# Three of a first tile's six transposing loads on ScalarE's queue, and a plan with other constants

## The chip, the core and the metric

The kernel runs on one core of a Trainium2 chip. The core's engines each run their own instruction stream, in order: TensorE (PE, with its weight loads as PEld), VectorE (DVE), ScalarE (ACT), GpSimd (POOL) and SyncE (SP). An engine waits on semaphores that other engines and the DMA transfers raise. SyncE and ScalarE can each issue DMA transfers from their own queue. The metric is the device time of one execution in microseconds (us).

## The reference

A speech codec's forward pass, in bfloat16: a depthwise convolution over time with three taps, SiLU, four stages of residual vector quantization with eight codes each, and a second depthwise convolution over the sum of the chosen codes. Shapes: x is 2 x 16000 x 512, dw_enc and dw_dec are 3 x 512, codebooks are 4 x 8 x 512.

```python
z = jnp.zeros_like(x)
for i in range(K):
    z = z + xp[:, i:i+T, :] * dw_enc[i][None, None, :]
z = _silu(z)
res = z
q = jnp.zeros_like(z)
for s in range(Nq):
    cb = codebooks[s]
    d2 = (jnp.einsum("btd,btd->bt", res, res)[..., None]
          - 2.0 * jnp.einsum("btd,cd->btc", res, cb)
          + jnp.einsum("cd,cd->c", cb, cb)[None, None, :])
    idx = d2.argmin(-1)
    sel = cb[idx]
    q = q + sel
    res = res - sel
qp = jnp.pad(q, ((0,0),(pad,pad),(0,0)))
y = jnp.zeros_like(x)
for i in range(K):
    y = y + qp[:, i:i+T, :] * dw_dec[i][None, None, :]
```

## The kernel before

**Tiles.** Each of the two sequences of 16000 rows is cut into nine tiles (SIZES, line 230): G = 6, 8 and seven of 16 groups of 128 rows for the first sequence, the mirror image for the second, 18 tiles in all. A tile's x lies in SBUF transposed, channels on the partitions, in one of two buffers XT (NX = 2): slot g + 1 holds the rows of group g, and slots 0 and G + 1 hold the neighbours that the convolution needs at the edges.

**Loading a tile** (load, lines 487 to 510). One transposing DMA for each of the G slots, all issued by SyncE (line 493). The edge slots of most tiles are two more such loads (lines 501 and 507), so a tile of 16 groups takes 18. For the first tile GpSimd makes the edge slots from slots G and 1 with two copies (lines 504 and 510).

**Setup** (lines 344 to 485). ScalarE's queue issues three small loads: the encoder weights WER, the codebooks CB1, and dw_dec, broadcast to all partitions. TensorE transposes WER, and VectorE copies it out as WENC, which the taps need. From the codebooks come their transposes CBT and CBM2 (ScalarE), Gram matrices and block tables BD (VectorE), and the stationary operands CBN; from dw_dec and the codebooks the decoder's tables WDEC. VectorE also clears a good many buffers at the start.

**One tile's work.** front (line 514): in each of two halves of the channels, three taps multiplied on ScalarE (line 531) or VectorE (line 532), two additions on VectorE, exp and reciprocal on ScalarE, and the product on VectorE (SiLU). select (line 582): scores on TensorE and decisions on VectorE for the first three stages. resid (line 681): the chosen codes are taken off z by TensorE products, and the result goes back to SBUF by ScalarE (line 707) or VectorE (line 709); then the fourth stage. back (line 741): the decoder as products on TensorE, copied out by ScalarE (line 766) and stored by SyncE (line 789).

**The order.** Nothing is scheduled by hand. Every step is registered with `add`, with its engine, a cost, a key of three numbers and what it reads and writes. `Plan.order` then simulates the engines with these costs: again and again it takes the step that can start earliest, and among steps that can start at the same time the one of the lowest rank. The rank is w[0] + key[1] + w[1] * key[2], with w from the table WHEN by the step's name and the part of the run (the first three tiles, the middle, the last three). The program's instructions are issued in that order, so it is each engine's order. A "tail" is the time from the end of a step's issue to its landing, as the plan counts it. SHARE and SLACK decide, where ScalarE and VectorE can both do a step, which of them does. The costs shape the order alone: the time on the chip is the chip's.

The DMA transfers share eight semaphores (numbers 101 to 108 in the trace), handed out in turn by the framework under the kernel. A transfer that gets a semaphore waits until that semaphore's earlier transfer has landed.

Of the kernel before, what the change touches and what calls it, by code (L numbers as in the profile page):

```python
# [12 lines left out]
ACT = mybir.ActivationFunctionType  # L13
# [3 lines left out]
class Plan:  # L17
# [9 lines left out]
    SPAN, BUSY = 3.413, 0.5  # L27
    GATE = {"resid": (1.0, 2.0), "back": (1.0, 2.0), "win0": (0.6, 1.5), "win3": (0.6, 1.5), "score0": (0.25, 1.4), "score3": (0.25, 1.4)}

    def __init__(self, pairs, edges, share, slack, quota, when):  # L30
        self.steps, self.writer, self.readers = [], {}, {}
        self.pairs, self.edges, self.share, self.slack, self.quota, self.when = pairs, edges, share, slack, quota, when

    def add(self, engine, cost, key, fn, reads=(), writes=(), take=None, free=None, hold=None, tail=0.0, after=(), dest=None, box=None, mm=0):
        n = len(self.steps)
# [18 lines left out]

    def rank(self, s):
        w = self.when[s["k"][0]][self.part(s)]
        return w[0] + s["k"][1] + w[1] * s["k"][2]

    def product(self, t, c, share, half):

# [14 lines left out]
    def order(self):  # L75
# [8 lines left out]
        at = [0.0] * len(steps)  # L84
        clock = {e: 0.0 for e in self.LATENCY}
        waiting = {e: [] for e in clock}
        held = {e: 0 for e in clock}
        banks = [0.0] * (2 * self.pairs)
# [4 lines left out]
        out = []  # L93
# [9 lines left out]
        def load(d, t):  # L103
            return max(clock[d] - t, 0.0) + held[d] + sum(cost(steps[m], d) for m in waiting[d]
                                                        if at[m] <= t + 1.0 and (d == "DVE" or not isinstance(steps[m]["e"], tuple)))
# [8 lines left out]
        def look(s, e):  # L114

            t = max(at[s["n"]], clock[e])
            if s["take"]:
                dest = s["dest"]
                if dest == "ANY":
                    full = [d for d in ("ACT", "DVE") if held[d] >= self.quota[d]]  # L120
                    if len(full) == 2:
                        return inf, None
                    if full:
                        dest = "ACT" if full[0] == "DVE" else "DVE"
                    else:
                        dest = "DVE" if load("DVE", t) + self.share[self.part(s)] < load("ACT", t) else "ACT"
                elif dest and held[dest] >= self.quota[dest]:
                    return inf, None
                kind = s["take"][0]
                t = place(kind[dest] if isinstance(kind, dict) else kind, t)[0]  # L130
                return t + late(many(s, dest), t, cost(s, dest) if s["dest"] == "ANY" else s["c"]), dest
            if isinstance(s["e"], tuple) and e == "ACT" and t + s["c"]["ACT"] > max(at[s["n"]], clock["DVE"]) + s["c"]["DVE"] + self.slack[self.part(s)]:
                return inf, None
            if s["mm"]:
                t += late(s["mm"], t, s["c"])
            return t, None
# [9 lines left out]
        while len(out) < len(steps):  # L146
            (t, dest), _, n, e = min(((look(steps[n], e), rank[n], n, e) for e, names in waiting.items() for n in names),
                                     key=lambda q: (q[0][0], q[1], q[2], q[3]))
            assert t < inf
            s = steps[n]  # L150
            for w in waiting.values():
                if n in w:
                    w.remove(n)
            c = cost(s, dest if s["take"] and s["dest"] == "ANY" else e)
            s["fill"] = None
            if s["mm"] and s["k"][0] != "setup":
                j = min(range(2 * self.pairs), key=lambda j: (banks[j], j))
                since = max(clock["PE"], banks[j])
                k = 0
                while t - clock["PE"] > self.AFTER and since + self.REST + self.FILL * (1 if self.full else 2) < t:  # L160
                    since = self.product(since, self.FILL, 1.0, 2.0)
                    k += 1
                if k > 0:
                    s["fill"] = (j, k)
                    run += k
                    if run > self.CHUNK:
                        run -= self.CHUNK
                        fetched = t + self.FETCH
            if s["take"]:
                kind, box = s["take"]  # L170
                kind = kind[dest] if isinstance(kind, dict) else kind
                j = place(kind, t)[2]
                box["banks"] = [j, j + 1] if kind == "A" else [j]
                for j in box["banks"]:
                    banks[j] = inf
                box["dest"] = dest
                if s["dest"] == "ANY":
                    steps[n + 1]["e"] = dest
                if dest:
                    held[dest] += 1  # L180
            elif s["box"] is not None:
                s["box"]["dest"] = e
            if s["hold"] and table != s["hold"]:
                table = s["hold"]
                c += self.TABLE
            if s["mm"]:
                m = many(s, dest)
                c = self.product(t, c, *self.GATE.get(s["k"][0], (0.5, 1.5))) - t
                run += m
                if run > self.CHUNK:  # L190
                    run -= self.CHUNK
                    fetched = t + c * (m - run) / m + self.FETCH
            s["t"], s["d"], s["on"] = t, c, e
            clock[e] = t + c
            self.busy[e] += c
            end = t + c + s["tail"]
            if s["free"]:
                if s["free"]["dest"]:
                    held[s["free"]["dest"]] -= 1
                for j in s["free"]["banks"]:  # L200
                    banks[j] = end + self.LATENCY[e]
            out.append(s)
            for u in users[n]:
                ue = steps[u]["e"]
                at[u] = max(at[u], t + c + self.AGAIN[e] if ue == e else end + self.LATENCY[e])
                left[u] -= 1
                if not left[u]:
                    open_(u)
# [5 lines left out]
def kernel(  # L214
# [8 lines left out]
    nc = tc.nc  # L223
# [18 lines left out]
    PAIR = 1  # L242
    NX, NE, NZ, NOH, NY = 2, 3, 4, 4, 4
    NA = 4
    SHARE = (19.5, 1.71, -1.34)
    SLACK = (0.8, -4.83, -5.72)
    QUOTA = {"ACT": 4, "DVE": 4}
    WHEN = {"setup": ((-0.05, 1.675), (0.613, 1.016), (0.464, 0.931)), "load": ((-2.074, 0.741), (-2.063, 0.601), (-2.58, 0.741)),
            "pad": ((-1.343, 0.11), (-1.736, 0.115), (-2.291, 0.134)), "taps": ((0.284, 0.643), (-0.413, 0.648), (0.441, 1.172)),
            "exp": ((0.672, 0.139), (0.624, 0.043), (0.853, 0)), "plus1": ((1.287, 0.521), (0.349, 0.234), (0.268, 0.646)),  # L250
            "recip": ((0.542, 0.819), (0.469, 0.213), (1.361, 0.627)), "gate": ((-0.104, 0.712), (0.552, 0.521), (1.523, 0.809)),
            "score0": ((-0.134, 0), (0.889, 0), (-0.19, 0)), "decide": ((1.83, 0.266), (-0.088, 0.293), (0.366, 0.69)),
            "win0": ((2.039, 0), (2.077, 0), (2.756, 0)), "resid": ((1.585, 0.742), (1.683, 0.632), (1.826, 0.993)),
            "score3": ((2.285, 1.086), (2.738, 0.327), (2.939, 1.624)), "decide3": ((1.327, 0.17), (2.815, 0.429), (3.624, 0.724)),
            "win3": ((3.135, 0.143), (3.003, 1.197), (2.818, 0.209)), "back": ((2.723, 0.576), (3.156, 1.159), (4.372, 0.628))}
    assert B == len(SIZES) and T >= GM * P and GM <= 16

    xf = x.flatten_outer_dims()
# [7 lines left out]
    tiles = []  # L266
    for b, sizes in enumerate(SIZES):
        done = 0
        for g in sizes:
            r = g * P  # L270
            t0 = max(0, min(done - 2, T - r))
            end = T if t0 + r >= T else t0 + r - 2
# [11 lines left out]
    CB1 = sb([NC, D], BF16, "CB1")  # L284
# [37 lines left out]
    CBN = {(s, u): sb([P, D], BF16, f"CBN{s}_{u}") for s in range(3) for u in range(2)}  # L322
    WDEC = [sb([P, D], BF16, f"WDEC{v}") for v in range(4)]

    plan = Plan(NA, (3, len(tiles) - 3), SHARE, SLACK, QUOTA, WHEN)
    add = plan.add

    def ps(box):
# [14 lines left out]

    wd_rows = bass.AP(tensor=dw_dec.tensor, offset=dw_dec.offset, ap=[[0, P], [D, K], [1, D]])
    add("ACT", 0.6, ("setup", -9, 0), lambda: nc.scalar.dma_start(out=WER, in_=dw_enc.rearrange("k (i p) -> (k i) p", p=P)), writes=["WER"], tail=1.6)
    add("ACT", 0.6, ("setup", -9, 0), lambda: nc.scalar.dma_start(out=CB1, in_=codebooks.flatten_outer_dims()), writes=["CB1"], tail=2.2)
    def load_wd():
        with nc.allow_non_contiguous_dma(reason="small weights"):
            nc.scalar.dma_start(out=WDBC, in_=wd_rows)
    add("ACT", 0.4, ("setup", -8, 0), load_wd, writes=[("Y", 3)], tail=5.5)  # L350
    add("POOL", 2.0, ("setup", -30, 0), lambda: make_identity(nc, IDENT), writes=["I"])

    def pool_memset(t, v, tok, cost, key):
# [133 lines left out]
    def load(st):  # L487
        n, G = st["n"], st["G"]
        X = XT[n % NX]
        src = xf[st["row0"]:st["row0"] + G * P, :].rearrange("(p g) d -> g p d", g=G)  # L490

        def one(g):
            nc.sync.dma_start_transpose(out=X[:, :, g + 1, :], in_=src[g])
        for g in range(G):
            add("SP", 1.56 if n < 2 else 1.36, ("load", n, 0.01 * g), lambda g=g: one(g), [], [("X", n % NX, g + 1)], tail=1.5)
        key = ("pad", n - 20 * (n == 0), 0)
        xe, xo = [("XE", n % NX)], [("X", n % NX, G + 1)]
        r0, t0 = st["row0"], st["row0"] % T
# [348 lines left out]
```

## Time and profile before

| | us |
|---|---|
| median of 8 runs | 731.6 |
| lowest and highest of the 8 | 729.9 and 734.07 |
| profiled execution, its time | 729.9 |
| the same, span from the first to the last instruction | 728.1 |
| VectorE busy in the first 100 us | 84.09 |
| VectorE busy from 100 to 700 us | 575.8 |
| VectorE busy in the last 28.1 us | 15.12 |

A profile row of the timeline gives the start in us from the span's start, the duration, the engine, the line of the kernel, the operation, what it writes and reads, and how many instructions are merged into the row; in brackets, how long the engine was idle before it and what ended the wait. "SPq" and "ACTq" are instructions of SyncE's and ScalarE's sequencers, DMA issues among them; their duration is that of the issue, and the landing comes later. A row of the view by stretches gives the stretch, its length, the busy time of each engine with its count, the granted clock of TensorE, the share of time that the 16 DMA engines were busy, and GB/s.

### The profile page before, as it was taken

Reading aid. Unit: us, or ns where it says so; the run is one execution under the profiler, and the core shown is the slowest. Engines: PE = TensorE matmul, PEld = TensorE weight load, DVE = VectorE, ACT = ScalarE, POOL = GpSimd, SP = SyncE. Lnnn points to the kernel's source line nnn. Section 1 sums busy time; section 2 is a strip of 40 time slices with the busy share of each in tenths; the row PEclk is TensorE's granted clock in tenths of the full one; section 3 lists DMA queues with packets and bytes.
Section 4 is the critical chain, followed back from the end, with each engine's and each line's share of the span. In section 5 each row is a group of like instructions: output and inputs, shape, how many; then the busy total and the mean of one; then the engine's idle time right before and its main releaser. Section 6 shows DMA issues by size and latency. Waiting matters only on the chain.

```text
span 728.1 us, 24317 instructions
## 1 busy us (share of the span) xinstructions
PE 584.0 (80%) x10656; PEld 288.7 (40%) x10725; DVE 675.0 (93%) x1258; ACT 658.5 (90%) x583; POOL 10.4 (1%) x35
## 2 busy tenths in 40 slices
PE   5977676887887886888787788877788897889995
PEld 2443243343443443434343434433444343444442
DVE  8779899999999999999999999999999999999993
ACT  6888998699999999899989999999899999999656
POOL 2000000000010000000000000000000010000000
PEclk9999899999999999999999999989999999999999
DMA  5444455525154353736544444542535141302316
GB/s 112 94 95 95 100 113 103 132 67 94 31 147 91 107 90 96 125 79 146 105 110 96 139 74 109 127 90 60 96 110 139 55 131 23 120 2 88 117 32 212
DMA packets 163968, 71.89 MB, mean 99 GB/s; under 512 B 155567, under 2 KB 155599, under 8 KB 163862
## 3 DMA queue, kind: packets, MB, share of 16 engines
q1 hardware_dynamic: 163646, 69.90, 40.7%
q8 instruction: 84, 1.38, 0.8%
q10 hardware_dynamic: 216, 0.43, 0.2%
q14 instruction: 22, 0.18, 0.1%
HBM read 0.43 MB, written 32.77 MB: 46 GB/s over the span
## 4 chain that ended last, share of the span: by engine, by line
DVE 53%; PE 28%; issue 8%; ACT 8%; DMA 2%; ACTq 0%; DVEq 0%
DVE ZB L709 12%; PE ps L701 8%; DVE ZB L364 7%; PE ps L700 7%; DVE TA L364 7%; DVE TB L532 7%; PE ps L567 5%; DVE TA L532 3%; DVE EX L539 3%; PE ps L758 3%; DVE OHW L678 2%; ACT YB L766 2%; PE ps L809 2%; ACT ZB L707 2%; ACT EX L549 1%
## 5 line engine op out<-in xcount | busy, mean ns | idle before, releaser
L701 PE MATMUL ps<-OHW,CBN 128*128 128x512 bf16 (+1 forms) x768 | 268.1, 386 | 20.6 <-DVE ZB L709 10.7
L707 ACT CAST ZB<-ps 128x1024 bf16<-128x1024 f32 (+2 forms) x296 | 253.4, 934 | 31.8 <-PE ps L701 30.1
L700 PE MATMUL ps<-ZB,IDENT 128*128 128x512 bf16 (+1 forms) x530 | 205.6, 388 | 31.6 <-ACT ZB L707 13.9
L709 DVE TENSOR_TENSOR ZB<-ZB,ps 128x1024 bf16<-128x1024 bf16 (+2 forms) x136 | 142.8, 1061 | 4.8 <-PE ps L701 4.3
L701 PEld LDWEIGHTS <-CBN 128*128 128x128 bf16 x768 | 74.7, 99 | 142.4 <-issue 77.0
L766 ACT CAST YB<-ps 128x1024 bf16<-128x1024 f32 x126 | 121.8, 1043 | 9.0 <-PE ps L762 4.2
L537 ACT ACTIVATE EX<-ZB 128x4096 bf16<-128x4096 bf16 (+2 forms) x36 | 115.1, 3197 | 8.5 <-DVE ZB L364 8.1
L549 ACT ACTIVATE EX<-EX 128x4096 bf16<-128x4096 bf16 (+2 forms) x36 | 114.7, 3195 | 0.2
L567 PEld LDWEIGHTS <-ZB 128*32 128x32 bf16 x8064 | 75.1, 95 | 54.9 <-issue 52.3
L567 PE MATMUL ps<-ZB 128*32 128x64 bf16 x8064 | 87.4, 197 | 8.3 <-issue 5.6
L532 DVE TENSOR_SCALAR TB<-XT,WENC 128x2048 bf16<-128x2048 bf16 (+2 forms) x139 | 92.4, 683 | 0.2
L809 PE MATMUL ps<-MSK,IDENT 128*128 128x512 bf16 x277 | 70.4, 401 | 14.9 <-issue 2.5
L758 PE MATMUL ps<-WDEC,OHW 128*128 128x512 bf16 x219 | 68.0, 387 | 14.7 <-DVE ZB L709 4.6
L700 PEld LDWEIGHTS <-IDENT 128*128 128x128 bf16 x530 | 53.0, 100 | 66.9 <-issue 14.8
L364 DVE TENSOR_TENSOR ZB<-ZB,EX 128x4096 bf16<-128x4096 bf16 (+2 forms) x36 | 72.6, 2018 | 3.6 <-ACT EX L549 3.6
L364 DVE TENSOR_TENSOR TA<-TA,TB 128x4096 bf16<-128x4096 bf16 (+2 forms) x36 | 72.7, 2020 | 1.0 <-ACT TB L531 0.6
L364 DVE TENSOR_TENSOR ZB<-TA,TB 128x4096 bf16<-128x4096 bf16 (+2 forms) x36 | 72.6, 2017 | 0.1
L532 DVE TENSOR_SCALAR TA<-XT,WENC 128x2048 bf16<-128x2048 bf16 (+2 forms) x70 | 46.7, 687 | 0.9 <-DMA out_dram<-YB 0.4
L809 PEld LDWEIGHTS <-IDENT 128*128 128x128 bf16 x294 | 28.8, 102 | 46.5 <-issue 18.7
L539 DVE TENSOR_SCALAR EX<-EX 128x4096 bf16<-128x4096 bf16 (+2 forms) x35 | 38.4, 1096 | 1.2 <-ACT EX L537 1.2
L758 PEld LDWEIGHTS <-OHW 128*128 128x128 bf16 x252 | 22.8, 98 | 41.5 <-issue 18.3
L672 PE MATMUL ps<-IDENT,OHA 128*32 128x128 bf16 x504 | 21.5, 223 | 9.8 <-DVE OHA L364 4.8
(100 smaller groups left out, 394.4 us busy)
## 6 DMA issues: line engine op xcount, KB each, us to landing
out_dram<-YB SPq DMA_DIRECT2D x33, 448.0 KB
out_dram<-YB SPq DMA_DIRECT2D x28, 512.0 KB
XT<-in_x_dram SPq DMA_TRANSPOSE x283
out_dram<-YB SPq DMA_DIRECT2D x30, 60.0 KB
out_dram<-YB SPq DMA_DIRECT2D x31, 2.0 KB
out_dram<-YB SPq DMA_DIRECT2D x2, 224.0 KB
YB<-in_dw_dec_dram ACTq DMA_DIRECT2D x1, 384.0 KB
out_dram<-YB SPq DMA_DIRECT2D x1, 384.0 KB
```

The costliest lines, as they stand in the source:

```text
L364: add("DVE", cost, key, lambda: nc.vector.tensor_tensor(out=out, in0=a, in1=b, op=op), reads, writes, **kw)
L532: lambda dst=dst, src=src, w=w: nc.vector.tensor_scalar(out=dst, in0=src, scalar1=w, scalar2=None, op0=ALU.mult),
L537: add("ACT", act(2 * R), ("exp", n, h), lambda: nc.scalar.activation(v(ex), Z, ACT.Exp, scale=-1.0), zt, [("EX", sl), "ACTTAB"], hold="E")
L549: nc.scalar.add_instruction(mybir.InstActivation(name=nc.get_next_instruction_name(), engine=mybir.EngineType.Activation, func=ACT.Reciprocal,
L567: nc.tensor.matmul(o[HB * q:HB * (q + 1), u * ZW:(u + 1) * ZW].rearrange("p (s c) -> p s c", s=2), lhsT=blk, rhs=both, start=False, stop=( ...
L700: nc.tensor.matmul(o, lhsT=IDENT, rhs=zg[:, k0:k0 + nk, :], start=True, stop=False)
L701: nc.tensor.matmul(o, lhsT=CBN[s, u][:, i * P:(i + 1) * P], rhs=W[:, k0:k0 + nk, PADC:PADC + P], start=not on_act, stop=True)
L707: nc.scalar.copy(zg, v)
L709: nc.vector.tensor_tensor(out=zg, in0=zg, in1=v, op=ALU.add)
L758: nc.tensor.matmul(o, lhsT=W[:, k, PADC:PADC + P], rhs=WDEC[u], start=True, stop=not wrap)
L766: add("ACT", act_psum(1024), key, lambda k=k, box=box, Y=Y, k0=k0: nc.scalar.copy(Y[:, 2 * (k - k0):2 * (k - k0) + 2, :].rearrange("p g d ...
L809: nc.tensor.matmul(PS[j // 2][:, 512 * (j % 2):512 * (j % 2) + NMK * ZW], lhsT=IDENT, rhs=MSK.rearrange("p u w -> p (u w)"), start=True, s ...
```

## The change

Of the first tile's six transposing loads, those of odd g (slots 2, 4 and 6) are issued by ScalarE; slots 1, 3 and 5 stay with SyncE. ScalarE's three have the key ("load", -8.5, 0.01 * (G - g)). The three small loads on ScalarE's queue keep their engine; the keys of two of them move from -9 to -8 and from -8 to -7.5. The plan counts every transposing load of a slot at 1.36 with a tail of 2.0, where it counted 1.56 for the first two tiles, 1.36 for the others, and a tail of 1.5.

Beside this the planner gets a tuple MARGIN, of whose four numbers three are 0 and the fourth lengthens the modelled time of TensorE's products by 3%, and a table NUDGE, which is empty. SHARE, SLACK and many entries of WHEN have new values.

```diff
     def rank(self, s):
         w = self.when[s["k"][0]][self.part(s)]
-        return w[0] + s["k"][1] + w[1] * s["k"][2]
+        return w[0] + s["k"][1] + w[1] * s["k"][2] + self.more(s["k"][0], s)
+
+    def more(self, name, s):
+        return self.nudge.get(name, (0,) * 99)[s["k"][1]] if s["k"][0] != "setup" and s["k"][1] >= 0 else 0.0
...
-                c = self.product(t, c, *self.GATE.get(s["k"][0], (0.5, 1.5))) - t
+                c = self.product(t, c * self.margin[3], *self.GATE.get(s["k"][0], (0.5, 1.5))) - t
...
-    SHARE = (19.5, 1.71, -1.34)
-    SLACK = (0.8, -4.83, -5.72)
+    SHARE = (13.44, 1.65, -1.13)
+    SLACK = (0.8, -4.83, -5.51)
     QUOTA = {"ACT": 4, "DVE": 4}
-    WHEN = {"setup": ((-0.05, 1.675), (0.613, 1.016), (0.464, 0.931)), "load": ((-2.074, 0.741), (-2.063, 0.601), (-2.58, 0.741)),
...
+    MARGIN = (0, 0, 0, 1.03)
+    WHEN = {"setup": ((-0.05, 1.675), (0.353, 1.016), (0.468, 0.931)), "load": ((-2.074, 0.741), (-2.063, 0.601), (-2.926, 0.741)),
...
+    NUDGE = {}
...
-    add("ACT", 0.6, ("setup", -9, 0), lambda: nc.scalar.dma_start(out=CB1, in_=codebooks.flatten_outer_dims()), writes=["CB1"], tail=2.2)
+    add("ACT", 0.6, ("setup", -8, 0), lambda: nc.scalar.dma_start(out=CB1, in_=codebooks.flatten_outer_dims()), writes=["CB1"], tail=2.2)
...
-    add("ACT", 0.4, ("setup", -8, 0), load_wd, writes=[("Y", 3)], tail=5.5)
+    add("ACT", 0.4, ("setup", -7.5, 0), load_wd, writes=[("Y", 3)], tail=5.5)
...
-        def one(g):
-            nc.sync.dma_start_transpose(out=X[:, :, g + 1, :], in_=src[g])
+        def one(g, engine):
+            engine.dma_start_transpose(out=X[:, :, g + 1, :], in_=src[g])
         for g in range(G):
-            add("SP", 1.56 if n < 2 else 1.36, ("load", n, 0.01 * g), lambda g=g: one(g), [], [("X", n % NX, g + 1)], tail=1.5)
+            other = n == 0 and g % 2 == 1
+            add("ACT" if other else "SP", 1.36, ("load", -8.5 if other else n, 0.01 * (G - g if other else g)),
+                lambda g=g, engine=nc.scalar if other else nc.sync: one(g, engine), [], [("X", n % NX, g + 1)], tail=2.0)
```

The other new entries of WHEN differ from the old by at most 0.4; the rest of the diff passes the two new tables into the plan and adds the zeros of MARGIN and NUDGE to the plan's times.

## The prediction

> **What bounds the kernel now.** I read the page's busy shares and slices first, then the busy time of each engine by stretches, then the timeline of the first 26 us, the chain of waits there, and last the timelines of SyncE's queue and of VectorE's taps.
>
> ```profile
> PE 584.0 (80%) x10656; PEld 288.7 (40%) x10725; DVE 675.0 (93%) x1258; ACT 658.5 (90%) x583; POOL 10.4 (1%) x35
> DVE  8779899999999999999999999999999999999993
> ```
>
> VectorE (DVE) sets the time: 675.0 us of a span of 728.1 us. Its 53 us of idle time lie at the start (the 8, 7, 7 of the first slices) and at the end. ScalarE, at 658.5 us, is close behind. So a change pays or costs what it does to VectorE's idle time, and a stretch by stretch view says how much there is:
>
> ```profile
> 0.00:13.10 13.10, 5.13 (x23) 2.32 (x24) 10.30 (x59) 7.92 (x34) 3.84 (x29) 1.00 0.57 119
> 18.50:52.00 33.50, 28.50 (x359) 14.21 (x361) 25.13 (x67) 27.28 (x30) 0.00 (x0) 1.00 0.50 96
> ...
> 100.00:200.00 100.00, 94.97 (x164) 0.98 0.43 87
> 200.00:300.00 100.00, 98.15 (x155) 0.98 0.47 111
> ...
> 500.00:600.00 100.00, 94.51 (x154) 0.95 0.42 107
> ```
>
> In the first two rows the third figure after the lengths is VectorE (10.30 us of 13.10), the fourth ScalarE (7.92); the rows of 100 us hold VectorE alone. Until the first taps start at 13.1 us VectorE idles only 13.10 - 10.30 = 2.8 us, for it has 10.3 us of setup to do meanwhile. That is nearly all that an earlier first tile could save ahead of the taps.
>
> ```profile
> 0.74 18.33 SPq L493 DMA_TRANSPOSE XT<-in_x_dram  x14
> 0.76 0.61 ACTq L345 DMA_DIRECT2D WER<-in_dw_enc_dram  x1
> 1.41 0.36 ACTq L346 DMA_DIRECT2D CB<-in_codebooks_dram  x1
> 2.35 0.19 PE L369 MATMUL ps<-IDENT,WER 12*128 12x12 bf16 x1 [2.35 <-DMA WER<-in_dw_enc_dram]
> 3.66 0.18 PEld L393 LDWEIGHTS <-CB 32*128 32x128 bf16 x4 [1.22 <-DMA CB<-in_codebooks_dram]
> 4.14 0.36 ACTq L349 DMA_DIRECT2D YB<-in_dw_dec_dram  x1
> ...
> 7.33 1.27 SPq L493 DMA_TRANSPOSE XT<-in_x_dram  x1
> ...
> 11.03 0.68 POOL L504 COPY XT<-XT 128x508 bf16<-128x508 bf16 x1 [4.85 <-DMA XT<-in_x_dram]
> 12.63 0.93 ACT L531 ACTIVATE TA<-XT,WENC 128x768 bf16<-128x768 bf16 x1
> 13.12 0.41 DVE L532 TENSOR_SCALAR TA<-XT,WENC 128x768 bf16<-128x768 bf16 x1
> 20.42 1.26 SPq L507 DMA_TRANSPOSE XT<-in_x_dram  x1
> ```
>
> SyncE's queue issues a load every 18.33 / 14 = 1.31 us. The first tile's sixth is issued at 7.33 and has landed when GpSimd copies from it at 11.03, 3.70 us later. The weights WER and CB, on ScalarE's queue, are there at 2.35 and 3.66 us, ahead of all use.
>
> ```profile
> 0.74 3.38 DMA XT<-in_x_dram
> 4.12 0.02 issue
> 4.14 3.94 DMA YB<-in_dw_dec_dram
> ```
>
> The chain of waits shows how the queues are tied: the first load takes 3.38 us from issue to landing, and only then does ScalarE's queue issue the dw_dec load, although it touches nothing of that load's. The eight shared DMA semaphores, handed out in turn, do that. A wait of one queue for a landing of the other, written by no line of the kernel, is thus something this program has.
>
> ```profile
> 46.03 1.26 SPq L507 DMA_TRANSPOSE XT<-in_x_dram  x1
> ...
> 51.99 1.42 DVE L532 TENSOR_SCALAR TA<-XT,WENC 128x2048 bf16<-128x2048 bf16 x2 [0.15 <-issue]
> ```
>
> The third tile's last load is issued at 46.03; undisturbed ones take 2.84 us to land (the seventh, issued at 8.64, by its semaphore's record in the trace), so it lands at 48.9, 3.1 us ahead of its first tap. The second tile's (20.42, landed 23.3) is 4.2 us ahead of its tap at 27.52. SyncE's load stream is back to back through these tiles, so a delay of the stream over 3.1 us reaches VectorE.
>
> **The change, part by part.**
>
> *Where the three loads go.* The plan takes the step that can start first, and among equals the lowest rank. At the start all of ScalarE's are equal. The loads' rank is -2.074 - 8.5 + 0.741 x 0.01 = -10.57 for slot 6, then slots 4 and 2; WER's is -0.05 - 9 = -9.05. So the loads do not go in behind WER: all three go ahead of WER, CB and dw_dec. SyncE's three are planned at the same times (both cost 1.36 in the plan), so the program alternates: ScalarE slot 6, SyncE slot 1, ScalarE 4, SyncE 3, ScalarE 2, SyncE 5.
>
> *What the two queues do to each other.* Nothing here shows two queues transposing at once: all 283 transposing loads are SyncE's. Ends: side by side, or each waiting for the landing of the one before it on the other queue. Side by side the last is issued at 0.74 + 2 x 1.31 = 3.36 and lands 2.84 to 3.70 later, at 6.2 to 7.1. In turn, with six landings in a row: 0.74 + 3.38 + 5 x (2.84 + 0.03 for the wait) = 18.5; with 3.70 for each of the five it is 22.6. I take in turn, 18.5, because the nearest row is the dw_dec load, held by this program until a landing on the other queue. Against 11.0 now, the first tile is complete 7.5 us later.
>
> The Trainium skill, "DMA: Bandwidth & Descriptors", section "Silent corruption: two transposing streams in flight at once", states that transposing loads of two queues in flight together can swap rows of each other's destinations, and that the later stream has to wait for the earlier one's full completion count. No run here shows that. By it, the side-by-side end is not one that a program may reach, and the first tile comes at 18.5, not at 6.2.
>
> *ScalarE's queue.* Its third load is fifth in the row: issued at 0.74 + 3.38 + 3 x 2.87 = 12.7, done issuing at 14.0. Behind it stand WER (issued 14.0, used 1.59 later by today's rows, 15.6), CB (14.6, used at 16.9 against 3.66 now), dw_dec (15.0, landed 3.94 later at 18.9 against 8.08), and then all of ScalarE's own setup, in order. Up to 13.1 us ScalarE idles 13.1 - 7.9 = 5.2 us now; after the change all but the table load (1.28) of the first 16.9, so 15.6: 10.4 more.
>
> *SyncE's queue.* The second tile's first load follows its third load of the first tile (issued in the row's last place, 15.6) at 16.9 instead of 8.64. The stream is 8.2 us late; with the 3.1 us in hand ahead of the third tile's taps, 5.1 us reach VectorE, even if nothing else did.
>
> *VectorE.* What needs neither x nor the codebooks (memsets, sums of the identity, WENC) is some 5.8 us (5.3 busy us up to 7.0 us of the timeline, and JM and JN). Up to 18.5 us it idles 12.7 us against 2.8 now: 9.9 more if nothing is won back. The idle 8.4 us of the stretch from 18.5 to 52 us (33.5 - 25.13) can win some back, as the setup not done yet may fill it, where the plan's order allows.
>
> So the front costs 5.1 (load stream) to 10.4 us (ScalarE). I take 7.5, the delay of the first tile itself, which lies in the middle.
>
> *The plan's constants.* Costs of 1.36 for each load, a tail of 2.0, products 3% dearer, and new shares, slacks and ranks reorder the other 600 us as well; the other margins are 0 and the nudges are empty, which add nothing. They remove no instruction of VectorE's but shift some evacuations between it and ScalarE. No row prices another order. The nearest: VectorE's idle time in stretches of 100 us goes from 1.85 to 5.49 us, about 1.4 us around their mean, so six other stretches would differ by some 1.4 x sqrt(6) = 3.5 us either way. I take 0. The new order also assumes the first tile at 3 x 1.36 + 2.0 = 6.1 us and the third, 31 loads in, at 44.2; by the above they come at 18.5 and 46.03 + 8.2 + 2.84 = 57.1, which speaks for a loss more than for a gain.
>
> **Sum.** Span 728.1 + 7.5 + 0 = 735.6; the 1.8 us around the span (profiled run 729.9) make it 737.4. The profiled run was 1.7 us under the median of 731.6; against the median, 739.1. The case's own range: 731.6 + 5.1 - 3.5 = 733.2 to 731.6 + 10.4 + 3.5 = 745.5.
>
> **Rivals.**
>
> *Side by side* (the faster side). The loads overlap, tile 1 is there at 6.2 to 7.1 and the load stream is 3 x 1.31 = 3.9 us ahead. For it: the queues issue independently, and DMA engines are half idle early (share 0.57). Against it: the weights come 3 x 1.27 = 3.8 us later, WENC not before 7.3, and VectorE has only 2.8 us of idle time to give. It gains at most 3.9, and 2.8 by that idle time: 728.8. It decides if no transposing load on one queue waits for a landing on the other.
>
> *One switch.* SyncE's three go first, ScalarE's three wait once: landed at 3.36 + 2.84 = 6.2, then 6.2 + 2 x 1.31 + 2.84 = 11.7, as late as today. For it: the order in which semaphores are handed out puts SyncE's first three loads ahead of WER today (dw_dec, third on its queue, got the ninth). Cost: the weights come after 10.1 us, and VectorE idles 11.7 - 5.8 = 5.9 against 2.8: +3.1, 734.7.
>
> *The re-planned rest outweighs the front.* VectorE idles 24 us between 100 and 700 us; with every stretch as good as the best (1.85), 600 us would give 13 us back; 10 back would make it 731.6 + 7.5 - 10 = 729.1. Against it: such an order would have to hold on the chip everywhere although it assumes the first tile 12 us too early.
>
> **How the numbers follow.** In turn 0.64, one switch 0.12, side by side 0.16, re-planned rest 0.08. The runs spread from 729.9 to 734.07, so less than about 0.3% (2.2 us) can't be told from no change. Slower by more: 0.60 + 0.08 + 0.01 + 0 = 0.69; within: 0.03 + 0.04 + 0.04 + 0.01 = 0.12; faster: 0.01 + 0 + 0.11 + 0.07 = 0.19. The predicted time is that of the likeliest, 739.1. The range reaches down to 728.0, so that most of the faster cases lie in it, and up to 746.0, just over the likeliest's own upper end.
>
> **What would show it.** Right: ScalarE's transposing issues stand ahead of WER; those of the two queues alternate some 2.9 us apart; GpSimd's copy L504 or the first taps start near 18.5; PE's L393 near 16.9; the second tile's loads start near 16.9; VectorE's idle time up to 18.5 us is near 12 us. Wrong: issues of both queues 1.3 us apart with taps before 10 us (side by side), or SyncE's three back to back and ScalarE's after 6 us (one switch). If the front is late as said and the time is not, VectorE's idle time between 18.5 and 52 us will have shrunk from 8.4 us, or the stretches of 100 us will be fuller than today's.

## The result: slower by 0.7%, from a loss twice the forecast one and a gain that was not forecast

The changed kernel takes 736.28 us (median of 11 runs, 734.73 to 738.02) against 731.24 us before (32 runs): a ratio of 1.0073, 95% interval 1.0055 to 1.0090, or 5.0 us. The prediction was 739.1 us, in a range of 728.0 to 746.0.

The page of the changed kernel, busy shares and VectorE's slices:

```profile
span 732.9 us, 24198 instructions
PE 570.5 (78%) x10589; PEld 283.8 (39%) x10663; DVE 670.5 (91%) x1257; ACT 661.0 (90%) x584; POOL 7.6 (1%) x35
DVE  2699899999999999999999999999997999998983
```

VectorE's busy time fell by 4.5 us (675.0 before), yet the span grew by 4.8: its idle time is up by 9.3 us, and the first two slices, now 2 and 6, hold it. The timeline of the front says what it waits for:

```profile
6.33 12.30 ACTq L499 DMA_TRANSPOSE XT<-in_x_dram  x3
18.66 0.79 ACTq L351 DMA_DIRECT2D WER<-in_dw_enc_dram  x1
19.85 0.43 ACTq L355 DMA_DIRECT2D YB<-in_dw_dec_dram  x1
20.60 0.17 DVE L376 CAST WENC<-ps 128x12 f32<-128x12 bf16 x1 [13.83 <-PE ps L375]
20.91 0.42 DVE L540 TENSOR_SCALAR TA<-XT,WENC 128x768 bf16<-128x768 bf16 x1
23.83 0.72 ACT L487 ACTIVATE YB<-YB,JM 128x512 bf16<-128x512 bf16 x1 [21.81 <-DMA YB<-in_dw_dec_dram]
24.46 0.92 ACT L539 ACTIVATE TA<-XT,WENC 128x768 bf16<-128x768 bf16 x1
25.41 0.96 DVE L370 TENSOR_TENSOR TA<-TA,TB 128x1536 bf16<-128x1536 bf16 x1 [3.30 <-ACT TA L539]
```

ScalarE's three loads take 12.30 us to issue. VectorE is idle for 13.83 us until WENC and starts its taps at 20.91 instead of 13.12. It then waits another 3.30 us for ScalarE's share of the taps: ScalarE's first step in order is L487, which needs dw_dec, the last load on its queue. The chain of waits, start and length, shows the row of loads:

```profile
3.40 2.83 DMA XT<-in_x_dram
6.33 2.72 DMA XT<-in_x_dram
9.06 2.79 DMA XT<-in_x_dram
11.88 2.73 DMA XT<-in_x_dram
14.62 2.78 DMA XT<-in_x_dram
17.42 1.21 ACTq L499
19.85 3.90 DMA YB<-in_dw_dec_dram
```

And the issues of SyncE's queue within it:

```profile
9.06 1.19 SPq L499 DMA_TRANSPOSE XT<-in_x_dram  x1
14.62 1.19 SPq L499 DMA_TRANSPOSE XT<-in_x_dram  x1
20.12 1.19 SPq L499 DMA_TRANSPOSE XT<-in_x_dram  x1
```

SyncE's three loads of the first tile go out 1.3 us apart; the last lands at 6.23. From there every load on one queue starts within 0.1 us of the landing of the one before it on the other: ScalarE at 6.33, SyncE at 9.06, ScalarE at 11.88, SyncE at 14.62, ScalarE at 17.42, SyncE at 20.12. SyncE's loads in that row are already the second tile's. By its semaphore's record the first tile's last load lands at 20.04 us, against 10.98 before.

The trace also records which semaphores an issue waits for. ScalarE's first transposing load waits for numbers 101, 102 and 103, which SyncE's three loads raise, and takes number 104. Up to 17.42 us each later load waits for the number of the one just before it and takes the next, up to 108. No transfer had used 104 to 108 before, so these waits are not the eight semaphores coming round again, which held the dw_dec load in the kernel before. They are waits of one transposing queue for the other.

The Trainium skill, "DMA: Bandwidth & Descriptors", section "Silent corruption: two transposing streams in flight at once", asks that the first transposing load of the later queue wait for the full completion of the earlier queue's; without that, it says, whole rows can land in the wrong columns of both destinations. (The prediction speaks of rows swapped between the destinations; the section does not say that.) The rows agree that this program has such waits, 2.7 to 2.8 us apart; that loads without them corrupt each other no run shows. Loads side by side were not tried, so their time stays unknown.

### The profile page after: what moved, and what is told of

Same layout as the page of the kernel before. It is cut to its first block, busy times and chain, and to the rows that moved or that the text cites. A ratio compares the mean times of both kernels' runs of the same rounds, so it can differ in the third digit from the quotient of the medians.

```text
span 732.9 us, 24198 instructions
## 1 busy us (share of the span) xinstructions
PE 570.5 (78%) x10589; PEld 283.8 (39%) x10663; DVE 670.5 (91%) x1257; ACT 661.0 (90%) x584; POOL 7.6 (1%) x35
## 3 DMA queue, kind: packets, MB, share of 16 engines
q8 instruction: 83, 1.36, 0.8%
## 4 chain that ended last, share of the span: by engine, by line
DVE 46%; PE 23%; ACT 15%; issue 12%; DMA 3%; ACTq 1%; SPq 0%; DVEq 0%
DVE ZB L717 12%; DVE ZB L370 9%; PE ps L709 6%; PE ps L575 5%; ACT ZB L715 5%; DVE TB L540 5%; PE ps L708 5%; ACT EX L557 3%; DVE TA L370 3%; PE ps L766 2%; DMA XT<-in_x_dram 2%; ACT EX L545 2%; PE ps L817 2%; ACT YB L774 2%; DVE TA L540 2%
## 5 line engine op out<-in xcount | busy, mean ns | idle before, releaser
L715 ACT CAST ZB<-ps 128x1024 bf16<-128x1024 f32 (+2 forms) x300 | 256.8, 937 | 27.1 <-PE ps L709 25.9
L717 DVE TENSOR_TENSOR ZB<-ZB,ps 128x1024 bf16<-128x1024 bf16 (+2 forms) x132 | 139.3, 1070 | 5.8 <-PE ps L709 5.0
L575 PEld LDWEIGHTS <-ZB 128*32 128x32 bf16 x8064 | 77.9, 97 | 52.6 <-issue 49.8
L575 PE MATMUL ps<-ZB 128*32 128x64 bf16 x8064 | 90.1, 200 | 6.2 <-DVE OHW L686 2.9
L540 DVE TENSOR_SCALAR TB<-XT,WENC 128x2048 bf16<-128x2048 bf16 (+2 forms) x142 | 94.3, 682 | 0.1
L766 PE MATMUL ps<-WDEC,OHW 128*128 128x512 bf16 x219 | 70.9, 401 | 14.4 <-ACT ZB L715 4.8
L708 PEld LDWEIGHTS <-IDENT 128*128 128x128 bf16 x535 | 53.0, 99 | 64.4 <-issue 10.5
L817 PE MATMUL ps<-MSK,IDENT 128*128 128x512 bf16 x205 | 55.5, 409 | 19.0 <-issue 7.9
L817 PEld LDWEIGHTS <-IDENT 128*128 128x128 bf16 x227 | 22.0, 103 | 42.3 <-issue 24.1
L569 PE MATMUL ps<-MSK,IDENT 128*128 128x512 bf16 (+1 forms) x55 | 21.9, 398 | 9.5 <-DVE PR L734 4.2
```

The lines of the kernel that those rows point to most:

```text
L540: lambda dst=dst, src=src, w=w: nc.vector.tensor_scalar(out=dst, in0=src, scalar1=w, scalar2=None, op0=ALU.mult),
L575: nc.tensor.matmul(o[HB * q:HB * (q + 1), u * ZW:(u + 1) * ZW].rearrange("p (s c) -> p s c", s=2), lhsT=blk, rhs=both, start=False, stop=( ...
L708: nc.tensor.matmul(o, lhsT=IDENT, rhs=zg[:, k0:k0 + nk, :], start=True, stop=False)
L715: nc.scalar.copy(zg, v)
L717: nc.vector.tensor_tensor(out=zg, in0=zg, in1=v, op=ALU.add)
L766: nc.tensor.matmul(o, lhsT=W[:, k, PADC:PADC + P], rhs=WDEC[u], start=True, stop=not wrap)
```

## The experiments

**The queue alone, under each set of orders.** The first kernel is the changed one with its plan as it is, but SyncE issues all six loads. Every engine's order of work is that of the changed kernel.

```diff
-                lambda g=g, engine=nc.scalar if other else nc.sync: one(g, engine), [], ...
+                lambda g=g, engine=nc.sync: one(g, engine), [], ...
```

> The changed kernel, with its plan untouched: the plan still thinks that ScalarE issues three of the first tile's loads, so every engine's order of work stays that of the changed kernel, but all six are issued by SyncE. Theory Q (the loads of the two queues wait for each other's landings, and that is what costs): the first tile lands near 11 instead of 20.0 us, the weights near 3, VectorE's idle time in the first 40 us falls from 19.2 to 8 to 11 us, and the time from 736.3 to 727 to 729 us, under the kernel before (ratio 0.994 to 0.998). Rival O (the new orders are what costs, the queues cost nothing that matters): the time stays at 735 to 737 (ratio 1.005 to 1.008).

721.74 us, ratio to before 0.9867 (0.9841 to 0.9892). Its timeline, at the first taps and at the first SiLU product:

```profile
11.17 0.42 DVE L540 TENSOR_SCALAR TA<-XT,WENC 128x768 bf16<-128x768 bf16 x1 [3.41 <-DMA XT<-in_x_dram]
27.05 0.96 DVE L370 TENSOR_TENSOR ZB<-ZB,EX 128x1536 bf16<-128x1536 bf16 x1
```

The taps start at 11.17 us and the product at 27.05; in the changed kernel these were 20.91 and 40.1:

```profile
40.11 0.96 DVE L370 TENSOR_TENSOR ZB<-ZB,EX 128x1536 bf16<-128x1536 bf16 x1
```

The stretches of the one-queue version: length, VectorE's busy time (instructions), granted clock, DMA share, GB/s:

```profile
0.00:40.00 40.00, 34.12 (x119) 1.00 0.51 104
40.00:100.00 60.00, 53.93 (x91) 0.86 0.51 102
```

The same stretches of the changed kernel:

```profile
0.00:40.00 40.00, 20.77 (x81) 1.00 0.38 84
40.00:100.00 60.00, 54.49 (x114) 0.87 0.47 95
```

VectorE idles 5.9 us of the first 40, where the changed kernel idles 19.2. TensorE's granted clock is not the difference: it is 1.00 in both in the first 40 us, and 0.86 against 0.87 in the next 60. So the queues cost 736.3 - 721.7 = 14.6 us, more than either theory had: theory Q's sign holds, its 7 to 9 us do not, and rival O falls. The second kernel does the opposite: the kernel before, its orders untouched, with three loads issued by ScalarE ahead of all else there.

```diff
         def one(g):
-            nc.sync.dma_start_transpose(out=X[:, :, g + 1, :], in_=src[g])
+            engine = nc.scalar if n == 0 and g % 2 == 1 else nc.sync
+            engine.dma_start_transpose(out=X[:, :, g + 1, :], in_=src[g])
...
-        for s in plan.order():
+        moved = lambda s: s["k"][0] == "load" and s["k"][1] == 0 and round(100 * s["k"][2]) % 2 == 1
+        steps = plan.order()
+        for s in [s for s in steps if moved(s)][::-1] + [s for s in steps if not moved(s)]:
```

> The kernel before with its plan and every engine's order of work untouched, but three of the first tile's loads (slots 2, 4, 6) issued by ScalarE ahead of all else there. The queues alone, with the old orders. Theory Q: landings as in the changed kernel (first tile near 20 us, weights at 20 to 24) and the cost that the orders of the changed kernel showed, 11 to 15 us: 742 to 747 us (ratio 1.015 to 1.022). Rival A (the old orders have enough slack at the front to take it up, as the forecast of 5.1 to 10.4 us had it): 736 to 741 (1.007 to 1.014).

746.85 us, 1.0204 (1.0150 to 1.0258): 15.4 us over the 731.5 of the kernel before, measured beside it. Two sets of orders, and nearly one price. Rival A, the forecast's 5.1 to 10.4 us, falls. The stretches of this kernel, with the busy time of PE, PEld, DVE, ACT and POOL between length and clock:

```profile
0.00:40.00 40.00, 15.45 (x72) 6.95 (x73) 19.56 (x81) 15.31 (x44) 3.76 (x29) 1.00 0.32 71
40.00:100.00 60.00, 45.99 (x535) 21.75 (x534) 47.94 (x106) 51.11 (x54) 0.00 (x0) 0.91 0.51 96
```

The first 40 us of the kernel before:

```profile
0.00:40.00 40.00, 33.25 (x113) 1.00 0.51 103
```

VectorE idles 20.4 us in the first 40, against 6.75 before, and the next 60 us win nothing back (12.1 idle, 9.2 before).

**Fewer changes of queue.** The first attempt made the second to fourth tiles' loads depend on the first tile, with the plan made anew.

```diff
+        if n in (1, 2, 3):
+            s0, s1 = ((0, G + 2), (8, G + 2), (10, G + 2))[n - 1]
+            add("POOL", 0.3, ("pad", n - 20, 0), lambda: nc.gpsimd.tensor_copy(X[:, 0, s0:s1, 0], XT[0][:, 0, 2, 0:s1 - s0]),
+                [("X", 0, 2)], [("XE", 1)] * (n == 1) + [("X", n % NX, g) for g in range(max(s0, 1), s1)])
```

> The changed kernel with three small GpSimd copies that make the second to fourth tiles' loads depend on the first tile's slot 2, so that SyncE has nothing to issue while ScalarE's three loads run: one change of queue instead of six. (The copies write slots that the loads then overwrite.) Both queues still share the work. Theory Q in its finer form (what costs is the number of landings in a row, not the second queue): the first tile lands near 11.8 instead of 20.0 us, the second tile's loads start near 12.5 instead of 20.1, the time falls by 4 to 8 us to 728 to 732 (ratio 0.996 to 1.001). If the second queue costs by itself, through the weights behind its loads (still issued after 10 us): 733 to 736 (1.002 to 1.006).

753.59 us, 1.0297 (1.0268 to 1.0325): a miss of over 20 us. The front came earlier, as expected (first taps at 13.0 us, first SiLU product at 32.0 instead of 40.1), but the plan was made anew with the new dependences, which redrew the orders of the whole run: VectorE idles 36.6 us between 100 and 700 us, 23.5 in the changed kernel. The experiment had changed two things. Repeated with the plan held, the dependence is put in only where the instructions are issued:

```diff
         def one(g, engine):
+            if n == 1 and g == 0:
+                nc.gpsimd.tensor_copy(X[:, 0, 1, 0:2], XT[0][:, 0, 2, 0:2])
             engine.dma_start_transpose(out=X[:, :, g + 1, :], in_=src[g])
```

> The changed kernel with its plan untouched; ahead of the second tile's first load, one GpSimd copy of 2 elements that reads the first tile's slot 2 and writes what that load then overwrites, so SyncE's later loads stand behind all of ScalarE's three: one change of queue, not six. Theory Q: the first tile lands near 11.8 us, the weights, still behind ScalarE's three loads, near 12.7 to 15.4; of the 14.6 us between the changed kernel (736.3) and the one-queue version with the same orders (721.7) some 8 to 10 come back: 726 to 729 us (ratio to before 0.993 to 0.998). If it is the second queue or the weights' lateness that costs and not the landings in a row: 732 to 736 (1.001 to 1.006).

726.71 us, 0.9942 (0.9916 to 0.9968), as theory Q had it. There are still two queues, and the tile lands at 11.84 us. With fewer landings in a row, two thirds of the loss (9.6 of 14.6 us) are gone. The weights gain too, as they stand behind ScalarE's loads: WER is issued at 10.2 us, against 18.7 in the changed kernel and 0.8 with one queue. So this run alone does not part the tile from the weights.

**Where the weights come in.** Two kernels with the plan of the changed one and its three small loads elsewhere: on SyncE ahead of its first loads, and on GpSimd at the start.

```diff
-... nc.scalar.dma_start(out=WER, ...   (also CB1 and WDBC)
+... nc.sync.dma_start(out=WER, ...     (nc.gpsimd in the other kernel)
...
-        for s in plan.order():
+        steps = plan.order()
+        for s in [s for s in steps if s["n"] < 3] + [s for s in steps if s["n"] >= 3]:
```

> The changed kernel with its plan untouched, except that the three small loads (WER, codebooks, dw_dec) are issued by SyncE ahead of its first loads. By the waits that this leaves, ScalarE's three loads run first, then SyncE's, so there is one change of queue and the weights are there by 3 to 8 us. Theory Q: the first tile lands near 11.8 us as in the one-switch version, and with the weights early too the time is 722 to 725 us (ratio 0.987 to 0.991), 3 to 5 under the one-switch version; the second queue itself costs nothing. If the second queue costs by itself: 727 or more.

724.56 us, 0.9901 (0.9874 to 0.9928). ScalarE's three loads ran first, and SyncE's began at 7.85 us, so the tile came later than the 11.8 expected: the first taps are at 13.4. The time is inside the 722 to 725 expected, but 2.2 us under the one-switch version, not 3 to 5. It is 2.8 us over the one-queue version, whose taps start 2.3 us earlier: the second queue costs about what the tile is late by.

> The changed kernel with its plan untouched, except that the three small loads are issued by GpSimd at the very start. The row of loads on the two transposing queues stays as in the changed kernel, so the first tile still lands near 20 us, but the weights are there by some 5 us. What the late weights cost beside the late tile: theory Q with the tile as the larger part: VectorE no longer waits 3.3 us for ScalarE's taps (25.41 in the changed kernel, near 21.5 here), setup fills some of the wait for the tile, the first SiLU product comes at 35 to 37 instead of 40.1 us, and the time is 730 to 733.5 (ratio 0.998 to 1.003). Rival W (the weights are the larger part of the 14.6 us): 722 to 728. Rival N (only the tile matters): 735 to 737.

733.31 us, 1.0018 (0.9997 to 1.0040): the tile 0.9 us later than in the changed kernel, the weights early. Its timeline:

```profile
7.20 12.29 ACTq L499 DMA_TRANSPOSE XT<-in_x_dram  x3
21.03 0.42 DVE L540 TENSOR_SCALAR TA<-XT,WENC 128x768 bf16<-128x768 bf16 x1 [13.96 <-DMA XT<-in_x_dram]
22.21 0.96 DVE L370 TENSOR_TENSOR TA<-TA,TB 128x1536 bf16<-128x1536 bf16 x1
36.90 0.96 DVE L370 TENSOR_TENSOR ZB<-ZB,EX 128x1536 bf16<-128x1536 bf16 x1
```

The wait between taps and sum is gone (22.21 against 25.41), and with it 3.0 us of time. Of the 14.6 us, the late weights are some 3 to 4, measured with the tile late as well, and the late tile is the other 11 or so. Rivals W and N both fall.

Together the kernels with held orders suggest a rule. The median time less the start of the first SiLU product, which is read from the profiled execution, is nearly the same for all kernels with the same orders:

| kernel | first product, us | median, us | difference |
|---|---|---|---|
| new orders, one queue | 27.1 | 721.7 | 694.6 |
| new orders, ScalarE's loads first, weights on SyncE | 29.7 | 724.6 | 694.9 |
| new orders, one change of queue | 31.6 | 726.7 | 695.1 |
| new orders, six changes, weights on GpSimd | 36.9 | 733.3 | 696.4 |
| changed kernel | 40.1 | 736.3 | 696.2 |
| old orders, one queue (before) | 26.9 | 731.2 | 704.3 |
| old orders, two queues | 43.2 | 746.9 | 703.7 |

Within each set of orders the difference varies by 1.8 us at most, while the first product moves by 13 to 16 us. So a us of delay at the front is about a us of time, and nothing later wins it back. The rule is no finer than that: the profiled execution with the weights on SyncE took 729.2 us, 4.6 above its median, and with the profiled executions' own times the five differences spread over 5.3 us.

**What the orders are worth.** By the table the new orders are some 9 us better than the old. Are the constants better as such? The constants of each version with the other's loads, plans made anew; in the first, only the last part of the diff and the keys of the small loads are applied to the kernel before, in the second only `other` changes in the changed kernel:

```diff
-            other = n == 0 and g % 2 == 1
+            other = False
```

> The kernel before, with its old constants and planner, and only the loads and the three small loads' keys changed as in the change; the plan is made anew with them. Theory Q: the front loses as in the changed kernel and nothing is given back by new constants: 737 to 742 us (ratio 1.008 to 1.014). Rival O: 729 to 733 (ratio 0.997 to 1.002).

> The changed kernel with its new constants, all six loads planned for SyncE and issued by it; the plan is made anew. Theory Q: no wait between queues, so the front is as before the change; with the 4.6 us that VectorE's busy time fell by, 725 to 730 us (ratio 0.992 to 0.998). If that fall belongs to one plan alone and not to the constants: 729 to 734 (0.997 to 1.003). Rival O: 735 to 738 (1.005 to 1.009).

The old constants with two queues: 737.89 us, 1.0087 (1.0059 to 1.0116), as theory Q expected. But 746.85, the same loads under the old orders, shows that the 737.89 hides a redrawn order 9 us better. The new constants on one queue: 739.14 us, 1.0106 (1.0079 to 1.0133), outside what theory Q allowed, and 1 us above rival O's 735 to 738. Rival O is not saved by it, since its cause (bad orders in the changed kernel) fell in the first experiment: in these runs the new constants help in the plan that they came with, and not in the one made for a single queue. Two more kernels change only what the plan believes: MARGIN from 1.03 to 1.0 in the one-queue version, and in the kernel before the loads' cost (1.36 for all) and tail (2.0).

> The one-queue version with the changed kernel's plan (721.7 us), with one constant of the plan set back: products 3% dearer becomes 0%. All orders are made anew. Theory L (an order's worth is chance: any change of a constant draws another one from a spread of some 20 us): 726 to 742 us, and VectorE's idle time between 100 and 700 us changes from 24 by several us. Rival C (the new constants are better as such, and one of them little matters): 720 to 725.

> The kernel before, with only what the plan believes of the loads changed as in the change (cost 1.36 for all, tail 2.0); same queue, same constants, same instructions in other orders. Theory L (each new order draws its own time): outside 729.5 to 733.5, anywhere from 724 to 742 us. Rival S (the old constants hold their worth under a small change of a cost): 729.5 to 733.5 (ratio 0.997 to 1.003).

728.62 us, 0.9963 (0.9938 to 0.9987), and 740.21 us, 1.0132 (1.0085 to 1.0179). Both times lie where theory L had them, and rivals C and S fall. Theory L's other sign failed: VectorE's idle time between 100 and 700 us stayed at 24.0 us with MARGIN at 1.0 (24.15 with 1.03). Five orders of the same work, all with one queue and the tile there at 11 us: 721.7, 728.6, 731.2, 739.1 and 740.2 us. What differs is seen in the busy rows of the pages, here the best and then the worst:

```profile
PE 579.3 (81%) x10663; PEld 283.5 (39%) x10663; DVE 671.1 (93%) x1257; ACT 660.8 (92%) x584; POOL 9.0 (1%) x35
```

```profile
PE 585.2 (79%) x10693; PEld 284.5 (39%) x10693; DVE 682.1 (93%) x1265; ACT 655.8 (89%) x576; POOL 8.7 (1%) x35
```

VectorE's busy time in the five is 671.1, 676.1, 675.0, 679.7 and 682.1 us: 11 of the 18.5 us between best and worst are busy time. Most of that, 7.8 us, is eight more evacuations of TensorE's products (the step of line 709 in the kernel before), which the plan gave to VectorE rather than ScalarE. The rest is idle time.

## Why the prediction was right, and where it was not

The direction was right, so was the wait that costs, and the time lies in the range. The 5.0 us measured against 7.5 forecast are close by luck: two terms of the sum were mis-sized and their errors nearly cancel.

- *In turn, not side by side: right, on a ground that was not the cause.* The choice rested on the dw_dec load, held by a semaphore that came round again. The waits in the row are others, of one transposing queue for the other, on semaphores not used before. Nor do the 18.5 us follow from the rule that the prediction cites beside them: the version with one change of queue has such a wait too, and its tile lands at 11.84. The order was not quite the forecast one. SyncE's three loads went first (as the rival "one switch" had it, from the order in which semaphores are handed out) and then the queues alternated (as the forecast had it), because the second tile's loads joined the row. The second tile's first load went out at 9.06 us, not at 16.9. The tile landed at 20.04 us (forecast 18.5). That these are close is partly luck: the forecast had six of the first tile's landings in a row, and the trace has three loads together, landed at 6.23, and then five landings, two of them the second tile's. The second tile's last load was issued at 29.20 us, 8.8 us late (forecast 8.2).
- *ScalarE's queue: right in kind, too short.* The forecast had its loads done issuing at 14.0 us and its work starting at 16.9, when the codebooks come; they were done at 18.6 and it started at 23.8, as its order begins with a step on dw_dec.
- *The front's cost, taken as 7.5 us of 5.1 to 10.4: the step that failed.* It measured 14.6 us under the new orders and 15.4 under the old. The forecast took the delay of the tile (7.5, really 9.1), let the late weights go beside it, and supposed that some of the idle 8.4 us between 18.5 and 52 us could be filled (6.2 are left in the changed kernel). VectorE idles 19.2 us in the first 40 us of the changed kernel and 5.9 in the one-queue version: 13.3 of the 14.6. In the next 60 us it idles 5.5 against 6.1. So next to nothing of the wait was made up, under either fixed order; whether another order could have filled it no run shows.
- *The plan's constants, taken as 0, 3.5 either way: mis-sized.* The new orders gave 731.57 - 721.74 = 9.8 us. The bound came from idle time between 100 and 700 us, and there the forecast was right: 24.15 us idle in the one-queue version, 24.17 before. (The prediction's first lines put all of VectorE's 53 us of idle time at the start and the end; these 24 lie between.) Of the profiled executions' spans, 8.6 us apart, the gain lies where it was not looked for: 3.9 us less busy time of VectorE, 3.1 less idle time from 40 to 100 us, and 1.6 less before and after. The rival that the re-planned rest outweighs the front came near in its gain and failed for the front's cost.
- *Side by side* did not happen: at each change of queue the trace has a wait for the other queue's landing.

The version that beats both kernels is the first experiment: the new plan with all loads on SyncE, 721.7 us, 1.3% under the kernel before.

## What to carry to other kernels

Before a transfer is moved to a second queue, ask what the two queues wait for in each other: here a load that took 1.3 us of one queue took 2.8 us when the queues alternated, and it pushed the small loads behind it too. In a program like this one, whose engines work in a fixed order, count a delay ahead of the first work at its full length unless a particular ready step is named that fills it. When a change also makes a plan draw new orders, hold the orders fixed to price the change, and price the orders by themselves: here they are worth up to 18.5 us with the same work.

## What was not expected of the hardware

The issue of one transposing load behind the other queue's landing took 1.19 to 1.29 us, as in one queue; only the wait differs, so the price of a change of queue is the landing, 2.7 to 2.8 us, less the 1.3 us that an issue takes anyhow. The dw_dec load took 3.90 us from issue to landing in the changed kernel and 3.94 before, but 5.07 when SyncE issued it at 1.58 us beside ScalarE's three transposing loads. Those three had landed only at 7.8 us, 1.6 us later than the three that start the changed kernel without it (6.2).
